# A fused attention and MLP kernel: no constant products in TensorE's early gaps

## The chip, the cores and the metric

The kernel runs on one core of a Trainium2 chip. The metric is the device time of one execution in microseconds (us), as the median of several runs. A profiled execution gives a trace, from which every row shown here is taken; its times count from the start of the span, the time between the first and the last instruction.

## The reference

Attention with a few extra "beacon" keys in front of a causal mask, for 8 batches of 8 heads, 576 queries, head size 64 and 16 beacon keys, then an MLP with a sigmoid GELU on the 4608 tokens. Cut to what is computed:

```
k_all = concat(beacon_k, k);  v_all = concat(beacon_v, v)
scores = q @ k_all.T / sqrt(64);  scores[future keys] = -1e9
a = softmax(scores);  x = a @ v_all            # tokens x 512
h = x @ w_in                                   # 512 -> 2048
out = (h * sigmoid(1.702 * h)) @ w_out         # 2048 -> 512
```

Inputs and output are float32; the kernel computes in float16 with float32 sums.

## The kernel before

The heads are worked in 16 sets of four (two sets for each batch). For a set, VectorE transposes q and k (L472), with the beacon keys cast and transposed ahead of them (L457, L465); TensorE makes the scores with four 32-row products side by side, each head in its own 32 rows, in two steps for the 64 channels (L506); ScalarE takes the exponential out of PSUM (L518); VectorE or GpSimd masks it (L529, L536); TensorE multiplies with the values and with ones for the row sums (L594); VectorE turns the sums into factors (L604 to L615) and writes the scaled result, the MLP's input, to xT (L628). The MLP's first product is L652 in its plain form and L854 in a form that shares products, the second L698 and L767.

The first five chunks of scores (the tiles named p) are made for two heads at a time, so that one half's exponential runs beside the other half's scores; from the sixth chunk on, all four heads lie in one tile (s). In the page, "x8" of L506 is the half of one such chunk.

The order of all work on every engine is written out by hand in the table ORDER. A small planner (Plan.run) replays this table with assumed durations and gives each step a planned start (o.start) and end; steps are then emitted by planned start. At the end of the kernel function a loop goes through the planned steps. Ahead of a TensorE step whose planned start lies before WARM (in planned nanoseconds), it works out how long TensorE would stand idle by the plan, and fills that time with products of a constant tile: `scrap`, a part of tB that is not used yet, which two fills on VectorE (L327) set to 1.7 and -0.6 in turn. These products go to one of the four PSUM tiles of the ring (u0 to u3), the one that the plan has free first, and nobody reads them. They are L1378 in the trace. FIRST is the planned time at which the first of them may begin, and COLS the width that the count n is worked out in.

```
n = int((2.0 if until > FIRST else 1.8) * (o.start - max(until, since + 200)) / COLS)
if n > 1:
    idle = psu.tile([P, 512], F32, tag=f"u{i}", name=f"u{i}")
    for size in (8, 4, 2, 1):
        x, w = (f32(scrap), 64 * size) if size > 2 else (scrap, 256 * size)
        for _ in range(n // size if size == 8 else n % (2 * size) // size):
            nc.tensor.matmul(idle[:, 0:w], x[:, 0:P], x[:, 0:w], start=True, stop=True)
```

For sizes 8 and 4 the tile is read as float32, 512 or 256 columns wide; for 2 and 1 as float16, 512 or 256 wide.

## Time and profile before

| | us |
|---|---|
| median of 3 runs | 321.59 (321.48 to 322.43) |
| the profiled execution, its own time | 321.53 |
| its span | 319.8 |
| TensorE busy | 312.3 (98%) |
| ScalarE busy | 219.7 (69%) |
| constant products (L1378) | 23, starting between 2.6 and 18.0 |

In the page and the answers of the trace, PE is TensorE's products, PEld its weight loads, DVE VectorE, ACT ScalarE, POOL GpSimd. A row of a timeline gives the start, the length, the engine, the line and the operation, the tile written and the tiles read, and in brackets the idle time before it with what ended that. A row with a count (x24) merges instructions of one kind that follow each other. A row of the waits gives who waited, for whom, the sum in us, how often, and the longest.

### The profile page before, as it was taken

What the parts mean: (1) busy time and instruction counts of PE and PEld (TensorE: products, weight loads), DVE (VectorE), ACT (ScalarE), POOL (GpSimd) and SP (SyncE); (2) the same over time, 40 slices, a digit from 0 to 9 for tenths busy, and PEclk for the clock granted to TensorE, in tenths of its full rate; (3) what the DMA queues carried; (4) which work ended last, traced back from release to release, by engine and by line L of the source; (5) the groups of instructions that cost most, each with busy time, mean ns of one, the idle gap of its engine ahead of it and who ended that gap; (6) DMA issues with size and microseconds to landing.
All of it is one profiled execution on the core that took longest, in us unless ns stands there. A gap on an engine that the chain in (4) does not pass through costs nothing.

```text
span 319.8 us, 9545 instructions
## 1 busy us (share of the span) xinstructions
PE 312.3 (98%) x4119; PEld 224.0 (70%) x4119; DVE 245.9 (77%) x481; ACT 219.7 (69%) x275; POOL 113.4 (35%) x178
## 2 busy tenths in 40 slices
PE   6999999999999999999999999999999999999995
PEld 2568855544875467754778877646888888888884
DVE  4769967886883988875788979888978975784673
ACT  1778986557766697698867686768779776665520
POOL 8768479660136603472084108420320000000000
PEclk9999999999999999999999999999999999999999
DMA  7999999992148951398085707710021000111112
GB/s 121 175 203 209 206 192 183 177 227 56 37 74 113 135 81 37 42 158 121 7 81 93 112 4 79 99 35 2 2 93 43 2 32 3 35 67 36 67 65 101
DMA packets 58219, 28.80 MB, mean 90 GB/s; under 512 B 41280, under 2 KB 53568, under 8 KB 58176
## 3 DMA queue, kind: packets, MB, share of 16 engines
q0 software_dynamic: 47552, 18.49, 49.6%
q1 hardware_dynamic: 10560, 9.69, 9.2%
q8 instruction: 32, 0.52, 0.7%
q14 instruction: 11, 0.09, 0.1%
q10 hardware_dynamic: 64, 0.01, 0.0%
HBM read 37.22 MB, written 9.44 MB: 146 GB/s over the span
## 4 chain that ended last, share of the span: by engine, by line
PE 94%; DMA 2%; ACT 2%; DVE 1%; issue 0%; POOL 0%; ACTq 0%; POOLq 0%
PE u L767 31%; PE u L652 26%; PE u L854 12%; PE u L594 10%; PE s L506 9%; PE u L698 5%; DMA qn<-in_q_dram 2%; PE p L506 1%; PE u L1378 1%; ACT E L518 1%; DVE osb L783 0%; ACT L674 0%; DVE qT L472 0%; POOL kn L416 0%; ACT g L674 0%
## 5 line engine op out<-in xcount | busy, mean ns | idle before, releaser
L518 ACT ACTIVATE E<-s 128x2048 f16<-128x2048 f32 (+3 forms) x59 | 90.7, 1552 | 35.6 <-PE s L506 32.9
L652 PE MATMUL u<-xT,w 128*128 128x256 f16 (+1 forms) x512 | 87.8, 326 | 0.1
L536 POOL TENSOR_SCALAR_AFFINE_SELECT E<-E 128x512 f16<-128x512 f16 (+3 forms) x78 | 49.1, 646 | 84.2 <-ACT E L518 84.1
L652 PEld LDWEIGHTS <-w 128*128 128x128 f16 x512 | 49.1, 98 | 32.8 <-issue 0.9
L674 ACT ACTIVATE g<-u 128x512 f16<-128x512 f32 x80 | 43.5, 599 | 16.1 <-PE u L652 15.5
L767 PEld LDWEIGHTS <-g 128*128 128x128 f16 x512 | 48.5, 98 | 7.5 <-issue 0.5
L783 DVE SCALAR_TENSOR_TENSOR osb<-u,osb 128x512 f32<-128x512 f32 x48 | 32.9, 686 | 24.9 <-PE u L767 19.0
L767 PE MATMUL u<-w,g 128*128 128x256 f16 x384 | 50.2, 273 | 0.0
L767 PEld LDWEIGHTS <-sA 128*128 128x128 f16 x384 | 36.5, 98 | 5.9 <-issue 0.8
L882 ACT ACTIVATE g<-u 128x512 f16<-128x512 f32 x48 | 27.0, 602 | 15.0 <-PE u L854 9.1
L506 PEld LDWEIGHTS <-kT 32*128 32x128 f16 x1088 | 22.5, 92 | 17.3 <-issue 11.1
L767 PE MATMUL u<-tB,sA 128*128 128x256 f16 x256 | 34.4, 273 | 0.0
L628 DVE TENSOR_TENSOR xT<-u,rz 128x352 f16<-128x352 f32 (+2 forms) x52 | 26.1, 521 | 7.8 <-PE u L594 7.0
L506 PE MATMUL s<-qT,kT 32*128 32x192 f16 (+14 forms) x992 | 30.9, 247 | 0.3 <-ACT E L518 0.3
L432 POOL DMA_DIRECT2D vb<-in_v_dram x32 | 27.8, 872 | 9.0 <-PE s L506 5.4
L594 PE MATMUL u<-E,vb 128*32 128x352 f16 (+8 forms) x928 | 27.7, 262 | 0.6 <-DVE osb L783 0.6
L594 PEld LDWEIGHTS <-vb 128*32 128x32 f16 (+1 forms) x928 | 20.1, 96 | 7.3 <-issue 3.6
L554 DVE TENSOR_TENSOR zs<-zs,E 128x1344 f16<-128x1344 f16 (+2 forms) x36 | 21.9, 608 | 0.9
L472 DVE STREAM_TRANSPOSE kT<-kn 128x576 f32<-128x576 f32 x16 | 20.1, 1258 | 2.3 <-DMA kn<-in_k_dram 1.8
L472 DVE STREAM_TRANSPOSE qT<-qn 128x576 f32<-128x576 f32 x16 | 19.8, 1239 | 1.9 <-DMA qn<-in_q_dram 1.0
L854 PEld LDWEIGHTS <-w 128*128 128x128 f16 x192 | 18.7, 98 | 2.3
L854 PE MATMUL u<-xT,w 128*128 128x256 f16 x144 | 20.1, 273 | 0.0
(76 smaller groups left out, 393.1 us busy)
## 6 DMA issues: line engine op xcount, KB each, us to landing
out_dram<-osb SPq DMA_DIRECT2D x36, 256.0 KB, 2.4
kn<-in_k_dram POOLq DMA_DIRECT2D x16, 288.0 KB, 6.3
qn<-in_q_dram POOLq DMA_DIRECT2D x16, 288.0 KB, 6.3
vb<-in_v_dram POOLq DMA_DIRECT2D x24, 128.0 KB, 5.6
w<-in_moe_w_in_dram POOLq DMA_DIRECT2D x8, 256.0 KB, 9.2
w<-in_moe_w_out_dram POOLq DMA_DIRECT2D x4, 512.0 KB, 11.8
vb<-in_v_dram POOLq DMA_DIRECT2D x8, 112.0 KB, 5.8
vb<-in_v_dram POOLq DMA_DIRECT2D x8, 80.0 KB, 6.0
```

The lines of the kernel that those rows point to most:

```text
L432: nc.gpsimd.dma_start(out=t[0 : hi - lo, j, h0:h1, :], in_=v[b, h0:h1, lo:hi, :].rearrange("h n d -> n h d"),)
L472: nc.vector.transpose(out=f32(dst.rearrange("p n e -> p (n e)")).rearrange("p (r t) -> p t r", t=TR), in_=f32(src[:, :]).rearrange("p (t c ...
L506: nc.tensor.matmul(u[:, o : o + w], kT[s % NB2][r : r + 32, j * P : (j + 1) * P, d], qT[s % NB2][r : r + 32, a : a + w, d], start=(d == 0) ...
L518: nc.scalar.activation(out=Es[s][:, h0:h1, c0:c1], in_=sall[(i, p)][:, :, o : o + c1 - c0], func=AFT.Exp, scale=0.125,)
L536: nc.gpsimd.affine_select(out=blk, in_=blk, compare_op=ALU.is_ge, fill=0.0, base=off + (Nb if j == 0 else 0), pattern=[[0, Q], [1, w]], ch ...
L594: nc.tensor.matmul(u[32 * h : 32 * h + 32, a:e], lhs, src[0:kw, h, col : col + e - a], start=first, stop=last, skip_group_check=s >= EARLY ...
L652: nc.tensor.matmul(u[:, o + a - t0 : o + e - t0], w1t[:, kp, nt * P : (nt + 1) * P], xT[:, kp, a % XR : (e - 1) % XR + 1], start=(kp == 0 ...
L674: nc.scalar.activation(out=gts[g][:, n0:n1, 0:w], in_=rings[("m1", g, n0)][:, 0 : n * w].rearrange("p (n w) -> p n w", n=n), func=AFT.Gelu ...
L767: nc.tensor.matmul(u[:, HM * mt : HM * (mt + 1)], lhs[:, n, mt * P : (mt + 1) * P], rhs[:, n, :], start=(n == 0 and mt == 0 and p not in ( ...
L783: nc.vector.scalar_tensor_tensor(out=osbs[(g, dst)][:, :], in0=rings[("p", g, p)][:, :], scalar=scale_of(g), in1=osbs[(g, src)][:, :], op0 ...
L854: nc.tensor.matmul(u[:, HM * n : HM * (n + 1)], lhs[x][:, (2 * i + n) * P : (2 * i + n + 1) * P], rhs[:, x, :], start=fresh and n == 0 and ...
L882: nc.scalar.activation(out=gts[g][:, n : n + 2, HM * h : HM * (h + 1)], in_=rings[src][:, :].rearrange("p (n w) -> p n w", n=2), func=AFT. ...
```

## The change

WARM goes from 20000 to 0. No planned start lies below 0, so the loop emits no constant products at all. The tile scrap is still filled, and the order of all other instructions on every engine stays the same.

```
     scrap = tB[0][:, 4:8, :].rearrange("p a n -> p (a n)")
     for i, x in enumerate((1.7, -0.6)):
         nc.vector.memset(scrap[:, i::2], x)
-    FIRST, WARM, COLS = 3800, 20000, 256
+    FIRST, WARM, COLS = 3800, 0, 256
...
     for o in order:
         if o.eng == "PE" and o.start < WARM:
```

More of the change, by code (lines that the diff above doesn't have):

```diff
@@ L327 @@
         nc.vector.memset(scrap[:, i::2], x)
-    FIRST, WARM, COLS = 3800, 20000, 256
+    FIRST, WARM, COLS = 3800, 0, 256
     def e_keep():
```

## The prediction

> **What bounds the kernel now.** I read the page's busy times and slices first, then the waits of TensorE alone behind the first stage, then TensorE's and ScalarE's timelines of the first 21 us.

> ```profile
> PE 312.3 (98%) x4119; PEld 224.0 (70%) x4119; DVE 245.9 (77%) x481; ACT 219.7 (69%) x275; POOL 113.4 (35%) x178
> PE   6999999999999999999999999999999999999995
> ```

> ```profile
> PE u L594 <- DVE osb L783: 0.6, 1, 0.6
> PE s L506 <- ACT E L518: 0.3, 1, 0.3
> ```

> The second fence is the whole list of TensorE's waits from 20 us to the end: 0.9 us in 300. Behind 21 us the kernel is TensorE's own work in a fixed order, with nothing to take up a delay, so whatever time the first stage gains or loses by then reaches the end one for one. My checkpoint is the second L652 burst, at 20.92 us: TensorE is busy without a wait from the score burst ahead of it.

> Next, what the constant products (L1378) do. These are TensorE's weight loads for the first group of them:

> ```profile
> 4.46 0.34 PEld L1378 LDWEIGHTS u<-tB 128*128 128x128 f32 x1 [0.52 <-issue]
> 5.32 0.34 PEld L1378 LDWEIGHTS u<-tB 128*128 128x128 f32 x1 [0.52 <-issue]
> 6.17 0.34 PEld L1378 LDWEIGHTS u<-tB 128*128 128x128 f32 x1 [0.52 <-issue]
> 6.82 0.19 PEld L1378 LDWEIGHTS u<-tB 128*128 128x128 f32 x1 [0.32 <-issue]
> 7.25 0.19 PEld L1378 LDWEIGHTS u<-tB 128*128 128x128 f32 x1 [0.24 <-issue]
> ```

> One and the same instruction pair starts every 0.85 us, then every 0.43, and the load itself falls from 0.34 to 0.19. TensorE runs at half speed up to about 6.6 us, that is for 4.0 us from its first product at 2.60, and at full speed from there. (The page's clock line shows 9 in that slice too, so the durations decide.) Last, the stage in which the other groups lie:

> ```profile
> 8.65 0.64 PE L506 MATMUL p<-qT,kT 32*128 32x288 f16 x24
> 9.22 1.34 PE L1378 MATMUL u<-tB 128*128 128x512 f32 x3
> 10.49 0.51 PE L506 MATMUL p<-qT,kT 32*128 32x288 f16 x8
> 10.94 0.70 PE L1378 MATMUL u<-tB 128*128 128x256 f32 x2
> 11.57 0.52 PE L506 MATMUL p<-qT,kT 32*128 32x288 f16 x8
> ```

> ```profile
> 9.34 3.60 ACT L518 ACTIVATE E<-p 128x1024 f16<-128x1024 f32 x4 [6.10 <-PE p L506]
> 13.12 5.01 ACT L518 ACTIVATE E<-p 128x1024 f16<-128x1024 f32 x6 [0.18 <-PE p L506]
> 18.96 1.45 ACT L518 ACTIVATE E<-s 128x1536 f16<-128x1536 f32 x1 [0.82 <-PE s L506]
> ```

> From 9.34 to 18 us ScalarE's exponentials run almost end to end: they set this stage's pace, TensorE feeds them, and the products fill its gaps (4.3 us busy between 8.6 and 20.4).

> **Part 1: what goes.** 23 products in eight groups (10, 3, 2, 2, 2, 1, 2, 1), nothing else; the fills of tB stay, 2 x 0.49 us on VectorE, done by 2.54, ahead of a wait for a DMA that ends at 3.35, so they cost nothing now or then. The first group ends as qT becomes ready (transpose 7.34 + 1.26 = 8.60), and the first real product starts at 8.65. Its removal alone moves no start. The other seven groups do sit on the path a little: at 11.28 the second exponential ends, but its next scores start at 11.57, behind products issued at 10.94. I put a number on that with the chain below run at full speed throughout: the checkpoint comes at 20.10, a gain of 0.82.

> **Part 2: what it costs.** Without the first group, TensorE meets its real work at half speed. Rules of the chain, all from rows: a burst occupies TensorE for its row's busy time less 0.16 (the latency of its last product: 0.59 long at a pitch of 0.43), twice that at half speed, with a latency of 0.21 (1.06 at a pitch of 0.85); 0.05 us between TensorE and ScalarE each way (the first scores end at 9.29, their exponential starts at 9.34); exponentials follow each other after 0.92, 0.90 (1024 wide) or 0.72 (768), and last 1.02 or 0.81; a half's next scores wait for that half's exponential. Order as in the timeline: scores 0 (both halves together), 1, 2 (a, b), two values bursts, scores 3, 4, three values bursts, scores 5, values, L652, scores 6, L652.

> The unknown is when full speed comes. Bounds from the row above, 4.0 us of work: in the chain TensorE starts at 8.65, stands from 9.61 to 10.94 for the exponential, and is then busy without a break. If every burst counts as those products did, full speed comes at 10.94 + 4.0 = 14.94. But a score burst of this stage works on two 32-row weights at once (x8 in pairs), 64 of 128 rows; counted by half, 10.94 to 14.83 gives 1.95, the values bursts to 15.79 give 0.96, and the last 1.09 take to 18.0. I know no row that is nearer to one of them and take the middle, 16.5. The chain then (start on TensorE; start of its exponential):

> ```
> scores 0   8.65-9.61   exp  9.87, 10.79      values x2   14.83-15.79
> scores 1a 10.94-11.66  exp 11.92             scores 3a,b 15.79, 16.51  exp 16.72, 17.44
> scores 1b 11.86-12.58  exp 12.84             scores 4a,b 17.58, 18.30  exp 18.16, 18.88
> scores 2a 12.79-13.81  exp 14.07             values x3   18.66-19.37
> scores 2b 13.81-14.83  exp 15.09             scores 5    19.74         exp 20.32
> values 20.11, L652 20.36, scores 6 at 21.82 (exp 20.32 + 1.45 + 0.05), L652 at 22.19
> ```

> Against the rows of before, the exponentials at 9.34, 13.12 and 18.96 come 0.53, 0.95 and 1.36 later, and the checkpoint 22.19 - 20.92 = 1.27 later. The same chain for other times of full speed: 12.2 gives -0.1, 14.94 +0.56, 15.9 +0.97, 18.0 +1.50, 20 +1.78, 24 +3.2, 27 +4.2.

> **Sum.** The profiled execution took 321.53 (span 319.8 and 1.7 around it), 0.06 under the median 321.59. 321.53 + 1.27 = 322.80, and set against the median 322.9: 0.4% slower. A measurement of this kernel can tell about 0.3%, 0.96 us, from no change; the chain reaches that when full speed comes at 15.9.

> [...]

> **Rivals.** (a) Not slower: full speed comes early, before 15.9, since broken or half-filled work counts in full. Its place is the exponentials' chain: once TensorE is at full speed, the gaps that the products no longer fill are given back, and the balance of this refund (0.82) against the half-speed bursts decides. At 14.94 it ends at +0.56, 322.15; at 13.4 at +0.2; at 12.2 it is past even, and below that it gains. For it: behind 10.94 the half-speed bursts leave no break. Against it: 64 rows of 128.
> (b) Late: half-filled bursts hardly count, or the thinner work of 15 to 20 us lets the speed fall back, and only the dense L652 bursts from 20 us on bring it. Full speed at 24 gives 321.59 + 3.2 = 324.8, at 27 325.8. For it: in no row of before does TensorE have to reach or hold full speed on scores alone. Against it: at half speed those bursts fill all of its time.
> (c) The speed does not depend on TensorE's work but on time since the start. Then the products only stood in the way, full speed is there at 8.65, and the checkpoint gains 0.82: 320.8. For it: one change of speed is all the trace has. Against: nothing in the trace speaks for a clock that knows the start.
> That the change might not do what it says is out: the changed program has 25 TensorE rows fewer, all of L1378, the same order elsewhere.

> **How the numbers follow.** Forecast, full speed from 15.9 to 20: 0.44, ending at +1.0 to +1.8. Rival (a) 0.26, (b) 0.20, (c) 0.10. Slower by over 0.3% is the forecast and (b), 0.64. Rival (a) lies within 0.3%, and so does (c) at its worked price of -0.82, just; I give half of (c) to faster, since the refund is a bound from one execution: same 0.31, faster 0.05. For the range, leaving out (c) and the later half of (b) leaves out 0.2: from -0.1 (321.5) to +3.3 (324.9). By itself the forecast's own range is 322.6 to 323.4.

> **What would show it.** In the profile after: no L1378; the first L506 burst at 8.65 about 1.1 us long instead of 0.64; exponentials at 9.87, 14.07 and 20.3; x8 score bursts near 0.9 long until full speed comes and 0.5 behind; the second L652 burst at 22.2; all behind it shifted by as much and no new wait. The forecast is wrong if the 24-product burst still takes 0.64 (then it is c), if bursts at 15.5 us already take 0.5 (a), or if L652's bursts of eight, 1.05 us long now, take 1.9 at 21 us (b).

## The result

The change makes the kernel slower: the median goes from 322.01 us (321.48 to 322.43, 4 runs) to 323.91 us (323.53 to 324.23, 4 runs), a ratio of 1.0060 with a 95% interval of 1.0046 to 1.0073. That is +1.9 us where +1.27 was forecast: above the forecast's own 322.6 to 323.4, inside the whole range. The two profiled executions lie further apart: 321.53 and 324.23, +2.70; the one of before is among the lowest of its kernel's runs and the changed one is the highest of its own. Two executions further down, one of before at 399.88 us (granted clock 0.756) and one of the run at 1.2 at 453.35 us (0.655), are left out of every comparison.

The page's busy times of the changed kernel, then TensorE's whole list of waits from the checkpoint (the second L652 burst, now at 23.62 us) to the end:

```profile
PE 307.4 (95%) x4096; PEld 223.0 (69%) x4096; DVE 246.6 (76%) x481; ACT 219.9 (68%) x275; POOL 113.2 (35%) x178
```

```profile
PE u L594 <- DVE osb L783: 0.6, 1, 0.6
```

Behind the checkpoint there is the same single wait as before, so the first stage's delay went to the end: 23.62 - 20.92 = 2.70 us at the checkpoint, 2.70 us between the executions. TensorE has 23 products fewer (4119 to 4096), not the 25 rows that the prediction counts in the program. The end of the first stage before:

```profile
18.77 0.41 PE L594 MATMUL u<-E,vb 128*32 128x288 f16 x12
19.11 1.05 PE L652 MATMUL u<-xT,w 128*128 128x256 f16 x8
20.92 1.05 PE L652 MATMUL u<-xT,w 128*128 128x256 f16 x8
```

And TensorE's timeline of the first stage now:

```profile
8.66 1.04 PE L506 MATMUL p<-qT,kT 32*128 32x288 f16 x24 [8.66 <-DVE qT L472]
10.80 3.67 PE L506 MATMUL p<-qT,kT 32*128 32x288 f16 x40 [1.11 <-ACT E L518]
14.40 0.62 PE L594 MATMUL u<-E,ones 128*32 128x288 f16 x12
14.84 0.61 PE L594 MATMUL u<-E,vb 128*32 128x288 f16 x12
...
17.10 1.52 PE L506 MATMUL p<-qT,kT 32*128 32x288 f16 x16 [0.69 <-ACT E L518]
...
21.26 1.89 PE L652 MATMUL u<-xT,w 128*128 128x256 f16 x8
23.08 0.60 PE L506 MATMUL s<-qT,kT 32*128 32x192 f16 x16
23.62 1.05 PE L652 MATMUL u<-xT,w 128*128 128x256 f16 x8
```

The first scores take 1.04 us instead of 0.64, values bursts 0.62 instead of 0.41, and the first L652 burst still 1.89 instead of 1.05. Only behind it does everything have its old length: TensorE stays at half speed up to 23.3 us. (The trace's clock record starts full speed at 23.32; such times below are taken from these records. Time ahead of the first record counts as full in the granted clock, which is 1.000 for this execution in spite of its 23.3 us at half speed: in these traces a mean below 1 tells of a later fall, not of a late start.) ScalarE's exponentials show the delay grow:

```profile
9.73 3.66 ACT L518 ACTIVATE E<-p 128x1024 f16<-128x1024 f32 x4 [6.49 <-PE p L506]
13.60 1.94 ACT L518 ACTIVATE E<-p 128x1024 f16<-128x1024 f32 x2 [0.21 <-PE p L506]
16.24 1.51 ACT L518 ACTIVATE E<-p 128x768 f16<-128x768 f32 x2 [0.70 <-PE p L506]
17.96 1.51 ACT L518 ACTIVATE E<-p 128x768 f16<-128x768 f32 x2 [0.21 <-PE p L506]
20.90 1.45 ACT L518 ACTIVATE E<-s 128x1536 f16<-128x1536 f32 x1 [1.43 <-PE s L506]
23.75 1.45 ACT L518 ACTIVATE E<-s 128x1536 f16<-128x1536 f32 x1 [1.40 <-PE s L506]
```

### The profile page after: what moved, and what is told of

It reads as the page before. It is cut to its first block, busy times and chain, and to the rows that moved or that the text cites. A ratio compares the mean times of both kernels' runs of the same rounds, so it can differ in the third digit from the quotient of the medians.

```text
span 322.5 us, 9499 instructions
## 1 busy us (share of the span) xinstructions
PE 307.4 (95%) x4096; PEld 223.0 (69%) x4096; DVE 246.6 (76%) x481; ACT 219.9 (68%) x275; POOL 113.2 (35%) x178
## 4 chain that ended last, share of the span: by engine, by line
PE 94%; ACT 2%; DMA 2%; DVE 1%; issue 0%; POOL 0%; POOLq 0%
PE u L767 31%; PE u L652 26%; PE u L854 11%; PE u L594 10%; PE s L506 9%; PE u L698 4%; PE p L506 2%; DMA qn<-in_q_dram 2%; ACT E L518 1%; DVE osb L783 0%; ACT L674 0%; DVE qT L472 0%; POOL kn L416 0%; ACT g L674 0%; POOLq L1399 0%
## 5 line engine op out<-in xcount | busy, mean ns | idle before, releaser
L518 ACT ACTIVATE E<-s 128x2048 f16<-128x2048 f32 (+3 forms) x59 | 90.7, 1552 | 36.9 <-PE s L506 34.3
L652 PE MATMUL u<-xT,w 128*128 128x256 f16 (+1 forms) x512 | 88.6, 328 | 0.1
L652 PEld LDWEIGHTS <-w 128*128 128x128 f16 x512 | 49.5, 98 | 33.1 <-issue 1.1
L783 DVE SCALAR_TENSOR_TENSOR osb<-u,osb 128x512 f32<-128x512 f32 x48 | 32.9, 685 | 24.9 <-PE u L767 19.0
L506 PEld LDWEIGHTS <-kT 32*128 32x128 f16 x1088 | 24.1, 96 | 26.8 <-issue 13.6
L506 PE MATMUL s<-qT,kT 32*128 32x192 f16 (+14 forms) x992 | 31.3, 249 | 0.0
L594 PE MATMUL u<-E,vb 128*32 128x352 f16 (+8 forms) x928 | 28.5, 268 | 0.6 <-DVE osb L783 0.6
L594 PEld LDWEIGHTS <-vb 128*32 128x32 f16 (+1 forms) x928 | 20.5, 98 | 7.6 <-issue 3.7
## 6 DMA issues: line engine op xcount, KB each, us to landing
w<-in_moe_w_out_dram POOLq DMA_DIRECT2D x4, 512.0 KB, 10.4
```

Of the source, the lines that this page charges most:

```text
L506: nc.tensor.matmul(u[:, o : o + w], kT[s % NB2][r : r + 32, j * P : (j + 1) * P, d], qT[s % NB2][r : r + 32, a : a + w, d], start=(d == 0) ...
L518: nc.scalar.activation(out=Es[s][:, h0:h1, c0:c1], in_=sall[(i, p)][:, :, o : o + c1 - c0], func=AFT.Exp, scale=0.125,)
L594: nc.tensor.matmul(u[32 * h : 32 * h + 32, a:e], lhs, src[0:kw, h, col : col + e - a], start=first, stop=last, skip_group_check=s >= EARLY ...
L652: nc.tensor.matmul(u[:, o + a - t0 : o + e - t0], w1t[:, kp, nt * P : (nt + 1) * P], xT[:, kp, a % XR : (e - 1) % XR + 1], start=(kp == 0 ...
L783: nc.vector.scalar_tensor_tensor(out=osbs[(g, dst)][:, :], in0=rings[("p", g, p)][:, :], scalar=scale_of(g), in1=osbs[(g, src)][:, :], op0 ...
```

## The experiments

All edits are against the kernel before. The median of before moved between 321.61 and 322.09 from chip to chip, so each run is compared with the runs of before that it shared its chip with.

### Only the first group

```
-    FIRST, WARM, COLS = 3800, 20000, 256
+    FIRST, WARM, COLS = 3800, 9000, 256
```

> Only the first group of constant products (ten, from 2.6 us to the first scores) is kept; the seven later groups go. Theory A (full speed has to be earned once by dense work, and the later groups only stand in the way): full speed near 6.6 us as before, the second L652 burst about 0.8 us earlier than 20.92, and the time 0.5 to 0.9 us below the kernel before. Rival B (the later groups hold the speed up, since the stage's own work is too thin): the speed falls back somewhere between 10 and 20 us, x8 score bursts take 0.9 instead of 0.5 again, and the time is 0.5 to 2 us above before. Rival C (speed does not depend on the work): as A.

323.30 us (323.08 to 323.82) against 322.09, ratio 1.0044 (1.0030 to 1.0059). Theory A is wrong, and rival B's fall came: the time lies 1.2 us above before. This is TensorE's busy time by stretches of 3.41 us (after the stretch and its length come PE, PEld, DVE, ACT, POOL, then the granted clock, DMA share and GB/s):

```profile
5.95:9.36 3.41, 2.87 (x31) 1.37 (x30) 2.19 (x3) 0.00 (x0) 2.39 (x3) 1.00 1.11 183
9.36:12.77 3.41, 1.70 (x40) 1.17 (x28) 3.38 (x8) 3.27 (x4) 3.06 (x8) 1.00 2.31 156
12.77:16.19 3.42, 3.03 (x57) 2.04 (x52) 1.91 (x7) 2.61 (x4) 2.50 (x4) 0.50 1.30 198
16.19:19.60 3.41, 3.03 (x60) 2.07 (x63) 1.64 (x5) 2.54 (x4) 2.30 (x4) 0.50 1.19 203
19.60:23.01 3.41, 3.41 (x56) 2.21 (x52) 2.73 (x7) 1.45 (x1) 1.36 (x4) 0.50 1.37 198
23.01:26.43 3.42, 3.42 (x80) 2.43 (x72) 1.49 (x3) 2.97 (x3) 2.02 (x4) 1.00 1.24 207
```

Full speed comes at 5.95, and falls back at 12.77 behind a stretch in which TensorE was busy half the time (1.70 of 3.41), all of it with 64-row scores apart from the end of the first burst. From there on it is the changed kernel again, up to 23.01. The two stretches at 0.50 with 3.03 of 3.41 busy did not bring the speed back.

### Only the later groups

```
-            if n > 1:
+            if n > 1 and until > FIRST:
```

> Only the first group goes; the 13 later products stay. Theory A: TensorE meets the first scores at half speed; the later products run at half speed too but fill the array's rows in the gaps, so full speed comes earlier than the 23.3 us of the changed kernel, at 13 to 20 us; time 0.5 to 2 us above before, below or level with the changed kernel. Rival B: since the later groups hold the speed up once it is there, they matter as much as the first, and the time lies well below the changed kernel's, under 1 us above before.

The runs fall in two parts: five at 322.92 to 324.13, and four at 327.8 to 328.9, of which there is no trace and which the ratio of 1.0043 (1.0029 to 1.0057) leaves out; the median of all nine is 324.13 against 322.09. In the profiled execution (323.20) full speed comes at 12.3, a little ahead of the 13 to 20 expected and eleven microseconds earlier than in the changed kernel:

```profile
9.64 2.50 PE L1378 MATMUL u<-tB 128*128 128x512 f32 x3
12.07 0.60 PE L506 MATMUL p<-qT,kT 32*128 32x288 f16 x8
```

The three products take 2.50 us instead of 1.34, push the second scores from 10.49 to 12.07, and bring full speed just there. So in this execution the later products brought the speed as well as held it, at the price of standing ahead of real work at half speed. That they cost over 5 us where full speed comes later is a guess at the four long runs that no trace shows.

### The first group with 64 rows

```
-    FIRST, WARM, COLS = 3800, 20000, 256
+    FIRST, WARM, COLS = 3800, 9000, 256
...
-    nc.tensor.matmul(idle[:, 0:w], x[:, 0:P], x[:, 0:w], start=True, stop=True)
+    nc.tensor.matmul(idle[:, 0:w], x[0:64, 0:P], x[0:64, 0:w], start=True, stop=True)
```

> As the run with the first group alone, but its ten products use 64 of the 128 rows (same widths, same number, same time on TensorE). Theory R (rows that stand empty count as idle, which is why the changed kernel's scores, 64 rows at once, did not bring full speed): no full speed by 8.65; the first score burst takes 1.04 us instead of 0.64 and the time is 1 to 2.7 us above before, like the changed kernel. Rival T (only the time that TensorE is busy counts): full speed at 6 to 8 us and a time like the run with the first group alone.

326.08 us (325.87 to 326.34), ratio 1.0127 (1.0112 to 1.0141). Theory R holds at this point, and the time is worse than I gave for it. TensorE's timeline:

```profile
2.59 7.83 PE L1378 MATMUL u<-tB 64*128 64x512 f32 x10 [2.59 <-DVE tB L327]
10.35 1.04 PE L506 MATMUL p<-qT,kT 32*128 32x288 f16 x24
```

7.8 us of unbroken work on 64 rows brings no full speed, where 4.0 us of it on 128 rows had before. All ten products run at half speed, end at 10.4, and hold up the first scores by 1.7 us; full speed comes at 25.6. Between this run and the one with the first group alone (full speed at 5.95) only the rows of the ten products differ: the time that TensorE is busy did not bring the rise by itself, and the rows at work mattered.

### The changed kernel again

> The changed kernel a second time. If full speed comes at the end of the first fixed slice of time that is dense enough, and the slices do not start with the kernel, then full speed comes at another time than 23.3 us here, between 20 and 24 us, and the time moves by half of that shift. If it is a fixed amount of work that counts, 23.3 us again within 0.1.

### Less fill

```
-    n = int((2.0 if until > FIRST else 1.8) * (o.start - max(until, since + 200)) / COLS)
+    n = int((1.4 if until > FIRST else 1.8) * (o.start - max(until, since + 200)) / COLS)
```

and the same with 1.0.

> First group as before; the later groups filled to 1.4 of the planned idle time instead of 2.0 (fewer products in the later groups). Theory B2 (the later products hold full speed by keeping the slices of 3.41 us dense in rows, and what they cost beside is the delay of real work queued behind them): the speed holds, the second L652 burst comes 0.1 to 0.4 us before 20.92, time 0.1 to 0.4 us below before. If the fill was just enough: a fall between 12 and 20 us as in the run with the first group alone, and +1 us or more in those executions.

> As the run at 1.4, but filled to 1.0 of the planned idle time. Theory B2: nearer to the run with the first group alone; I expect the speed to fall in at least part of the executions and the time 0.3 us below to 1.3 us above before. If it holds full speed, 0.4 to 0.7 us below.

At 1.4: 321.54 us (320.92 to 321.78) against 322.04, ratio 0.9979 (0.9971 to 0.9988): a gain of half a microsecond, a little over what I expected, and no run above before's median. In the profiled execution the speed comes late, at 8.07, but holds. At 1.0: 322.46 (321.19 to 324.05), ratio 1.0017 (1.0001 to 1.0033): the lowest run gains as expected. The six runs from 322.47 up have a mean granted clock of 0.981 to 0.989, four more 0.994 or 0.995, and two, the profiled one among them, 0.997 and 1.0. By an estimate, one slice at half speed takes off about 0.005 (half of 3.41 us in 321), and the three slices of the first group alone gave 0.984: so in those six the speed fell back for two slices or more, and in the four probably for one. Theory B2 holds in this kernel: without the later products it is 1.2 us slower than before, and with fewer of them 0.5 us faster.

### The data, and 64 rows in the later groups

```
-    for i, x in enumerate((1.7, -0.6)):
+    for i, x in enumerate((0.0, 0.0)):
```

> The kernel before with the constant tile filled with 0.0 instead of 1.7 and -0.6: the same products of zeros. If only which rows and when are counted: full speed near 6 us, held, time level with before. If the data count (products of zeros as idle): like the changed kernel or worse, 1.5 us or more above before, with the first scores late since the products ahead of them run at half speed.

321.96 us against 322.04, ratio 0.9997 (0.9988 to 1.0006): products of zeros make no difference that these runs show. The profiled execution is its longest (322.53): full speed came at 8.8 only, the first group at half speed ran past the first scores, and these started at 9.6. That is where the spread of the kernel before (321.5 to 322.5) comes from as well, as far as one trace of that kind shows.

```
+                r = 64 if until > FIRST else P
...
-    nc.tensor.matmul(idle[:, 0:w], x[:, 0:P], x[:, 0:w], start=True, stop=True)
+    nc.tensor.matmul(idle[:, 0:w], x[0:r, 0:P], x[0:r, 0:w], start=True, stop=True)
```

> First group as before, the later products use 64 of 128 rows (same widths and number). Theory R (the share of rows counts): less dense slices; the speed falls back between 10 and 20 us as with the first group alone or holds only just; time 0.5 us or more above before where it falls. Rival T (busy time counts): held, level with before.

321.87 us, ratio 0.9996 (0.9987 to 1.0005), held in the trace from 5.96 to the end: of theory R only "holds only just" is left, and rival T foresaw it too, so this run alone does not tell which measure decides the hold. Products on 64 rows brought no full speed in 7.8 us of the run above, and with them it was held here.

An estimate puts this in one number for a slice of 3.41 us: the share of the array that was at work. Each product is counted with its time (256 columns of float16 take 0.109 us at full speed, which is L652's pitch in 24 products of 2.79, and 0.213 at half, a quarter of the 0.85 between two float32 products of 512; float32 takes twice that) times the rows and columns of its weights over 128 x 128, the largest weights in the traces. Worked out so from the traces:

| estimate | at half speed, no rise behind it | at half speed, rise |
|---|---|---|
| before | 17% | 95% |
| changed kernel | 25, 27, 60, 56% | 88% |
| the same again | 21, 26, 64, 49% | 87% |
| first group alone | 56, 61% (behind the fall) | 93%, later 89% |
| later groups alone | 6% | 84% |
| first group, 64 rows | 34, 49, 49, 34, 53, 71% | 85% |
| zeros | 77% | 100% |

In the four traces further down the rise comes behind 90 to 100%. At full speed, the one slice of the first stage that ended in a fall has 16% (first group alone, 9.36 to 12.77). The ends of the traces show more of them, since TensorE is done some microseconds before the last output is written: there the speed falls behind slices of 15% (fill 1.4), 23% (zeros), 30% (fill 1.0) and 36% (the early fill below, at 1.4), and holds through slices of 40% (later groups alone), 43% (first group with 64 rows) and 44% (first group alone). The thinnest that held in the first stage have 38% (fill 1.0) and 39% (later groups with 64 rows).

Busy time does not put these in order. TensorE is busy for 1.70 us in the slice that fell in the first stage, and for less in this end slice of the later groups alone, behind which the clock stays at 1.00 (columns as for the first group alone):

```profile
316.08:319.49 3.41, 1.53 (x15) 1.13 (x12) 1.21 (x2) 0.00 (x0) 0.00 (x0) 1.00 0.49 173
319.49:322.90 3.41, 0.00 (x0) 0.00 (x0) 0.00 (x0) 0.00 (x0) 0.00 (x0) 1.00 0.17 58
```

In the early fill at 1.4 the end slice ends in a fall:

```profile
314.32:317.73 3.41, 1.38 (x13) 0.99 (x11) 1.05 (x2) 0.00 (x0) 0.00 (x0) 1.00 0.54 190
317.73:319.56 1.83, 0.00 (x0) 0.00 (x0) 0.00 (x0) 0.00 (x0) 0.00 (x0) 0.50 0.21 76
```

So of the slices counted here, those at half speed have no rise behind them up to 77% and have one from 84%; those at full speed have a fall behind them up to 36% and none from 38%. These are estimates from fourteen traces with a count of my own, good to about one per cent, and they stand for this kernel's traces alone. That rows matter for the rise is shown by experiment (the first group on 64 rows and on 128), and that busy time does not decide the hold by these slices (a fall behind 1.70 us, none behind 1.53); the measure that does is not shown.

### Earlier and thinner fill

Before, the first group has 6.05 us from its start at 2.60 to the first scores at 8.65, less than two slices (6.83), so a whole slice of it need not fit. If the rise comes behind one whole dense slice, as in the traces above, and the group began about 1 us earlier, one would always fit, and full speed by 8.65 would not depend on where the slices lie. Two runs fill the tile by one instruction ahead of VectorE's other fills:

```
+    scrap = tB[0][:, 4:8, :].rearrange("p a n -> p (a n)")
+    nc.vector.memset(scrap, 0.0)
     nc.vector.memset(bkf[:, 0:1, :], 0.0)
     nc.vector.memset(bkf[:, 1:HS, :], 0.0)
```

> The later groups at 1.4, and the constant tile filled with zeros by one instruction ahead of VectorE's other fills, so that the first group starts about 1 us earlier. If the spread of the run at 1.4 (320.9 to 321.8) comes from executions in which full speed arrives late and the first group, still at half speed, runs past the first scores' 8.65 us, then those executions go: scores at 8.65 in the trace, median 0.3 to 0.6 us below the run at 1.4, 0.7 to 1.1 below before. If the beacon load that the fill now delays by about 0.5 us is on the path: no gain over the run at 1.4.

> As the other run of this call, the later groups at 1.2. If the slices still hold the speed: 0.1 to 0.2 us below it. If some do not: a wider spread, up to 2 us above before as at 1.0, and a median above the run at 1.4.

At 1.4: eleven runs at 321.26 to 321.58 and one at 325.48 with a mean granted clock of 0.979, ratio 0.9994 (0.9972 to 1.0017), unclear. At 1.2: four runs at 321.14 to 321.17 with a clock of 1.0, seven at 324.4 to 325.4 with 0.976 to 0.982, ratio 1.0054 (1.0020 to 1.0089), slower. By their clock the speed fell back in the long ones; no trace shows where. At 1.4 the spread of the others did shrink, but the second branch of my expectation came true, by more than I gave for it. VectorE's timeline before, then at 1.4:

```profile
3.35 0.28 DVE L457 CAST bkn<-bkf 128x64 f16<-128x64 f32 x1 [0.81 <-DMA bkf<-in_beacon_k_dram]
```

```profile
6.23 0.53 DVE L456 CAST bkn<-bkf 128x64 f16<-128x64 f32 x1 [4.29 <-DMA bkf<-in_beacon_k_dram]
```

The cast of the beacon keys waits for its loads up to 6.23 instead of 3.35: a fill of 0.48 us ahead of the two small fills that those loads wait for (these start at 1.43 and 1.50 instead of 0.89 and 0.96) delayed the cast by almost three, and the first scores start at 9.43. So the fill was put behind the two fills that the beacon loads wait for, with the later groups at 1.4 and at 1.7:

```
     nc.vector.memset(bkf[:, 0:1, :], 0.0)
     nc.vector.memset(bkf[:, 1:HS, :], 0.0)
+    scrap = tB[0][:, 4:8, :].rearrange("p a n -> p (a n)")
+    nc.vector.memset(scrap, 0.0)
```

> The single early fill now stands behind the two small fills that the beacon loads wait for, and ahead of the rest; later groups at 1.4. Beacon loads as before (cast near 3.4 us, not 6.2), first product near 1.7 us, first scores at 8.65 in most executions, second L652 burst near 20.3; median 0.5 to 1.0 us below the kernel before. If the shorter waits leave slices too thin: single executions with a fall, 2 to 4 us longer.

> As the other run of this call, the later groups at 1.7: denser slices, real work delayed more. Median 0.1 to 0.4 us above it, and no execution with a fall.

At 1.4: 320.83 us (320.68 to 320.95) against 321.61, ratio 0.9972 (0.9961 to 0.9982). At 1.7: 320.70 (320.50 to 321.25), ratio 0.9973 (0.9962 to 0.9984). Both beat the kernel before by 0.3%, and the changed one, measured on other chips, by about 0.9%; the two cannot be told apart, so the price that I expected of the denser fill does not show, and no run of either shows a fall of a slice by its mean granted clock (0.997 to 1.0; in the trace of the first early fill, 0.997 came from its end alone). At 1.7:

```profile
1.67 5.62 PE L1377 MATMUL u<-tB 128*128 128x512 f32 x10 [1.67 <-DVE tB L322]
8.54 0.64 PE L505 MATMUL p<-qT,kT 32*128 32x288 f16 x24 [1.26 <-DVE qT L471]
9.12 1.13 PE L1377 MATMUL u<-tB 128*128 128x512 f32 x2
...
20.36 1.05 PE L651 MATMUL u<-xT,w 128*128 128x256 f16 x8
```

The products start 0.9 us earlier, end 1.3 us ahead of the scores, and the checkpoint comes at 20.36 instead of 20.92.

## Why the prediction came out as it did

The sign, the cause of the loss (real work at half speed until full speed comes) and the way to the end were right. What brings full speed, and so its time, the term that carried the sum, was not: what came is rival (b), to which the prediction gave 0.20. That the median moved by 1.9 us, not far from 1.27, is in part luck. Of the 2.70 us between the profiled executions, 0.48 is missing because the median of before, 322.01, lies above the execution that the sum started from, and 0.32 because the changed kernel's execution is its longest.

**What bounds the kernel.** Right. The checkpoint's delay reached the end in full, and no new wait came up.

**The first group.** Right that its removal moves no start (first scores at 8.65, now 8.66) and that it is what brought full speed (at 6.6 before, at 5.95 with it alone). But it is half of what the products do in this kernel: alone it is 1.2 us slower than before (323.30 against 322.09), since the speed fell back at 12.77, behind a slice of 16% by the estimate. Rival (c), a speed that does not depend on TensorE's work, fell with the first row: 1.04 instead of 0.64.

**When full speed comes.** This is the step that failed. I took the middle, 16.5 us, of a bound that counts 64-row bursts in full (14.94) and one that counts them by half and adds up (18.0); it came at 23.3. The bound itself was built wrongly: I let half-filled work add up until 4.0 us of full work were together. (I also took TensorE to be busy without a break behind 10.94; the trace has a stop of 0.69 us ahead of 17.10.) The traces do not show it adding up: in the changed kernel the four slices of 25, 27, 60 and 56% by the estimate are together 5.7 us of full work, more than the 4.0, and brought no full speed; it came behind the next one, of 88%, in which the first L652 burst lies. The 13.4 us among rival (a)'s times is an assumed one that no run shows; the changed kernel's two traces have 23.32 and 23.00. That is rival (b)'s cause, dense L652 work bringing full speed, at a time somewhat under the 24 to 27 us that I had priced for it, and its sign came true: L652's burst of eight took 1.89 us at 21.26.

**The price at half speed.** Too high, and this hid part of the miss. I doubled every burst; but a burst of scores grew from 0.64 to 1.04, or 1.73 times without the last product's latency (0.48 to 0.83 us, taking 0.16 and 0.21 off). The exponentials of the first chunks therefore came earlier than I had them: 9.73, 11.66, 12.58, 13.60 and 14.52 in the trace against 9.87, 11.92, 12.84, 14.07 and 15.09. By the forecast's chain, full speed at 23.3 would have cost about 2.9 us at the checkpoint (between its +1.78 for 20 and +3.2 for 24); it cost 2.70.

**The refund.** 0.82 us for the gaps that the later products hold up. It is there in part: with the beacon loads in order and fill at 1.4, the checkpoint stands at 20.16, 0.76 earlier than before, of which the first scores' own start is 0.11. But it can't be had by leaving the later products out. I took for granted that full speed, once there, stays; the run with the first group alone showed it falling back in the gaps (at 12.77). The prediction had that only as a half-sentence in rival (b).

## What to carry to other kernels

In this kernel the fill of constant products was worth what it did for the clock, and its two jobs asked for different amounts: full speed came behind slices of 84% and more by the estimate above, and 7.8 us of products with half the rows did not bring it, while it was held through slices of 38%. So fill the wait before the first real work densely and early, thin out the fill between the real bursts until single runs begin to fall back, and look at the spread and the granted clock of the runs as well as at the median, since where the slices lie changed from run to run (full speed at 23.32 and at 23.00 in the changed kernel); the granted clock showed a fall (0.984 with the first group alone), but not a late start (1.000 in the changed kernel). Before moving a small fill ahead of others, see which load's issue waits behind it: here 0.48 us of fill delayed the cast of the beacon keys from 3.35 to 6.23.

## What the runs showed that was not expected

In these traces the speed of TensorE rose only behind slices with 84% or more of the array at work by the estimate, and not behind one of 77%, while it was kept through 38% and not through 36%; with products of zeros the time was level (321.96 against 322.04). And half a microsecond more of fill ahead of the small beacon loads' own had the cast that waits for them start at 6.23 us instead of 3.35.
